# Batch 0's attention by pairs of chunks: other load order, weight-queue gate, and first-GEMM order in a fused attention + MLP kernel

## The chip, the core and the metric

The kernel runs on one core of a Trainium2 chip. The core has five engines, each with its own instruction queue worked strictly in order: TensorE (PE), VectorE (DVE), ScalarE (ACT), GpSimd (POOL) and SyncE (SP). Transfers between HBM and on-chip memory (SBUF) are done by 16 DMA engines; SP, ACT and POOL issue them. Matmul results land in PSUM, from where DVE or ACT copy them to SBUF.

The metric is the device time of one execution in microseconds. Before the change it is 290.98 us, the median of 13 runs (290.07 to 292.09).

## What is computed

```python
# q, k, v: (8 batches, 8 heads, 576 positions, 64), float32
q_s = exp(q - max) / sum over the 64 features
k_s = exp(k - max) / sum over the 576 positions
kv  = einsum('bhsd,bhse->bhde', k_s, v)
att = einsum('bhsd,bhde->bhse', q_s, kv)
x   = att.transpose(0, 2, 1, 3).reshape(4608, 512)
h   = x @ w_in            # 512 x 2048
out = maximum(0.01*h, h) @ w_out   # 2048 x 512
```

A linear attention: the softmax of q runs over features, that of k over positions, so each head needs only a 64 x 64 matrix `kv`. Its output feeds a two-layer MLP with a leaky ReLU.

## The kernel before

**Layout.** The four chunks `g` (0 to 3) of q, k and v hold two heads each: 128 partitions (two heads x 64), and in each partition nine groups `r` of 64 values, which are consecutive rows of the sequence. A pair of chunks, `gp` = 0 or 1, is the unit of most steps. The MLP works on nine token tiles `t` of 512 tokens (`TT`), batches have 576, so a batch always spans two tiles; batch 0's last 64 columns belong to tile 1.

**Attention of one batch**, per pair: `make_exp` (L157) takes the exponential of q or k on ACT; `make_qnorm` (L176) sums, inverts and scales q on DVE; `make_transpose` (L203) turns q with 64 x 64 matmuls on PE into a PSUM tile `pt` and copies it to `qT`; `make_vcast` (L167) casts v to bf16 with a column of ones beside it; `make_kv` (L225) sums k^T v over the nine groups in PSUM and then divides by k's sum (its inner `finish`, L241, two DVE instructions) into `kd`; `make_out` (L271) multiplies `kd` with `qT` and copies the result as columns of `xT`, the transposed input of the MLP.

**The MLP of one tile**, `emit_moe` (L429): first GEMM, 64 matmuls of 128 x 128 by 128 x 512 at L379 (16 blocks `j` of the hidden dimension, four contraction blocks `cb` each), two `j` to a PSUM tile `ph`, which ACT turns into `g_sb` with the leaky ReLU (L434); second GEMM, 64 matmuls at L388, into `pout`; a DVE copy (L405) and stores on SP's queue (L399). For tile 0 the first four `j` are done with `cb` outermost, and the second GEMM with `j` outermost, so that each quarter of `w_out` is only needed when its turn comes.

**Order.** Everything is written out by hand: each engine executes its instructions in the order in which the program emits them. `first_attn` (L329) prepares batch 0; then tiles follow. Pieces of the next batch's attention are put into `slots_of(t)` (L481): key (1, j) stands after block `j` of the first GEMM, key (2, ..) after a block of the second. `dummies` (L149) are matmuls on zeros, into a scratch tile, that keep PE active in the opening.

**Loads.** Batch 0 comes on SP's queue in six half loads (L84): q, k, v, each first chunks 0 and 1, then 2 and 3. All weights come on POOL's queue, which also casts them from float32 to bf16 on the way; the small copy `gate` (L128) holds that queue until the last half of k is there. Behind it stand four quarters of `w_in` (by 512 columns), then batch 1's q, two quarters of `w_out`, batch 1's k, a quarter of `w_out`, batch 1's v, the last quarter of `w_out`, and batch 2. Batches 3 to 7 are loaded on SP's queue, behind the stores of an earlier tile. PSUM is one pool of four double banks (`pair`, L70), used in turn.

Of the kernel before, what the change touches and what calls it, by code (L numbers as in the profile page):

```python
# [18 lines left out]
def kernel(  # L19
# [57 lines left out]
    def new_ld(st):  # L77
        for nm in "qkv":
            st[nm] = ld_pool.tile([P, NG, R * D], FP32, name=f"{nm}_ld", tag="ld")

    def load(eng, st, b, nm, g0=0, g1=NG):
        flat = dram[nm][b].rearrange("h s d -> (h s d)")
        src = flat.rearrange("(g p f) -> p g f", g=NG, p=P)[:, g0:g1, :]
        eng.dma_start(out=st[nm][:, g0:g1, :], in_=src)  # L84

    states = {b: {} for b in range(B)}
    new_ld(states[0])
    for nm in "qkv":
        for g0 in (0, 2):
            load(nc.sync, states[0], 0, nm, g0, g0 + 2)  # L90

    wsrc = const_pool.tile([P, TT], BF16, name="wsrc")
    nc.vector.memset(wsrc, 0.0)  # L93
# [19 lines left out]
    FQ = F // WQ  # L113
    JQ = NF // WQ

    def emit_w_in(i):
        f0, f1 = i * FQ, (i + 1) * FQ
        nc.gpsimd.dma_start(out=w_in_sb[:, :, f0:f1], in_=w_in_r[:, :, f0:f1])  # L118

    def emit_w_out(i):  # L120
        nc.gpsimd.dma_start(
            out=w_out_sb[:, i * JQ : (i + 1) * JQ, :], in_=w_out_r[:, i * JQ : (i + 1) * JQ, :]
        )

    gate = const_pool.tile([P, 1], FP32, name="gate")
    nc.gpsimd.tensor_copy(out=gate, in_=states[0]["k"][:, NG - 1, 0:1])  # L128
    for i in range(WQ):
        emit_w_in(i)  # L130
    new_ld(states[1])
    load(nc.gpsimd, states[1], 1, "q")
    emit_w_out(0)
    emit_w_out(1)
    load(nc.gpsimd, states[1], 1, "k")
    emit_w_out(2)
    load(nc.gpsimd, states[1], 1, "v")
    emit_w_out(3)

    def load_batch(eng, b):  # L140
        new_ld(states[b])
# [58 lines left out]
            for lo in (0, HP):  # L200
                yield par, 2 * gp + par, lo, (HP - lo if par else lo)

    def make_transpose(st, b, gp, r0=0, r1=R, copy=None):  # L203
        def piece():
            if "qT" not in st:
                st["qT"] = qT_pool.tile([P, NG, S], BF16, name="qT")
            pt = pair("pt", BF16)
            for r in range(r0, r1):
                for par, g, lo, to in quads(gp):
                    nc.tensor.matmul(  # L210
                        pt[to : to + HP, par, r * D : (r + 1) * D],
                        lhsT=qe_buf[b % 2][lo : lo + HP, g, r * D : (r + 1) * D],
                        rhs=ident[lo : lo + HP, lo : lo + HP],
                        is_transpose=True,
                        start=(r == r0),
                        stop=(r == r1 - 1),
                    )
            (copy or nc.vector.tensor_copy)(  # L218
                out=st["qT"][:, 2 * gp : 2 * gp + 2, r0 * D : r1 * D],
                in_=pt[:, :, r0 * D : r1 * D],  # L220
            )

        return piece
# [34 lines left out]
    def kv_piece(st, b):  # L258
        return lambda: make_kv(st, b)()()
# [39 lines left out]

        return piece  # L300

    def out_pieces(b, extra=()):
        n1 = TT - (b * S) % TT
        if 2 * n1 <= TT:
            groups = [[(b, gp, 0, n1) for gp in range(NP)]]
            groups += [[(b, gp, n1, S)] for gp in range(NP)]
        else:
            groups = [[(b, gp, 0, n1)] for gp in range(NP)]
            groups += [list(extra) + [(b, gp, n1, S) for gp in range(NP)]]
        return [  # L310
            make_out(parts, (nc.scalar.copy if i == 1 else nc.vector.tensor_copy,))
            for i, parts in enumerate(groups)
        ]
# [12 lines left out]
    def transpose_pieces(b, st):  # L326
        return [make_transpose(st, b, gp) for gp in range(NP)]

    def first_attn(st):  # L329
        b = 0  # L330
        acopy, dcopy = nc.scalar.copy, nc.vector.tensor_copy
        dummies(22)
        make_exp(st, b, "q", 0)()
        make_exp(st, b, "q", 1)()
        make_exp(st, b, "k", 0)()
        make_qnorm(st, b, 0, 0, R - 1)()
        make_qnorm(st, b, 1, 0, R - 1)()
        make_transpose(st, b, 0, 0, R - 1, acopy)()
        dummies(10)
        make_exp(st, b, "k", 1)()  # L340
        make_vcast(st, b, 0, 2, acopy)()
        make_vcast(st, b, 2, 3, acopy)()
        make_transpose(st, b, 1, 0, R - 1)()
        make_vcast(st, b, 3, NG)()
        dummies(3)
        kv0, kv1 = make_kv(st, b, [0]), make_kv(st, b, [1])
        fin0 = kv0()
        dummies(2)
        fin1 = kv1()
        fin0()  # L350
        fin1()
        dummies(2)
        for gp in range(NP):
            make_out([(b, gp, 0, TT)], (acopy, dcopy))()


    def rest_norm(st):
        for gp in range(NP):
            make_qnorm(st, 0, gp, R - 1)()
# [67 lines left out]
                store_rows(eng, t, tsub, lo, out_sb, o0, o1)  # L427

    def emit_moe(t, slots):  # L429
        x = xT.pop(t)  # L430
        g_sb = g_pool.tile([P, NF, TT], BF16, name="g_sb")

        def act(jj, ph):
            nc.scalar.activation(  # L434
                out=g_sb[:, 2 * jj : 2 * jj + 2, :], in_=ph, func=AF.Prelu, alpha=LEAKY_SLOPE
            )

        def run(*key):
            for piece in slots.get(key, ()):
                piece()  # L440

        JJ0 = 2 if t == 0 else 0
        if JJ0:
            phs = [pair("ph") for _ in range(JJ0)]
            for cb in range(NB):
                for j in range(2 * JJ0):
                    gemm1_mm(phs[j // 2], x, j, cb)
            for jj in range(JJ0):
                act(jj, phs[jj])
        for jj in range(JJ0, NF // 2):  # L450
            ph = pair("ph")
            for j in (2 * jj, 2 * jj + 1):
                for cb in range(NB):
                    gemm1_mm(ph, x, j, cb)
                if j % 2:
                    act(jj, ph)
                run(1, j)
        if t == 0:
            pouts = [pair("pout") for _ in range(NTS // 2)]
            for j in range(NF):  # L460
                for tsub in range(NTS):
                    gemm2_mm(pouts[tsub // 2], g_sb, tsub, j)
                run(2, j)
            for i in range(NTS // 2):
                store(pouts[i], t, 2 * i, 2 * i + 2)
        else:
            for tsub in range(NTS):
                if t == NT - 1 and tsub == NTS - 1:
                    last_subtile(g_sb, t, tsub)
                    continue  # L470
                alone = t == NT - 1 and tsub == NTS - 2
                if tsub % 2 == 0:
                    pout = pair("pout")
                for j in range(NF):
                    gemm2_mm(pout, g_sb, tsub, j)
                if tsub % 2 or alone:
                    store(pout, t, tsub if alone else tsub - 1, tsub + 1)
                run(2, tsub)


    def slots_of(t):  # L481
        slots = {}

        def put(key, pieces):
            slots.setdefault(key, []).extend(pieces)

        if t == 0:
            st, st0 = states[1], states[0]
            prep = prep_pieces(1, st)
            tr = transpose_pieces(1, st)  # L490
            outs = out_pieces(1, [(0, gp, TT, S) for gp in range(NP)])
            put((1, 5), [lambda: rest_norm(st0)])
            put((1, 13), prep[0:2])
            put((1, 15), prep[2:4])
            put((2, 4), prep[4:6])
            put((2, 6), [lambda: rest_transpose(st0), tr[0]])
            put((2, 10), prep[6:7])
            put((2, 11), [kv_piece(st, 1), tr[1]])
            put((2, 13), outs[0:2])
            put((2, 14), outs[2:3])  # L500
            return slots
        if t == 1:
            st = states[2]
            prep = prep_pieces(2, st)
            for i in range(7):
                put((1, 2 * i + 1), prep[i : i + 1])
            put((2, 0), transpose_pieces(2, st) + [kv_piece(st, 2)])
            outs = out_pieces(2)
            put((2, 2), outs[0:2])
            put((2, 3), outs[2:3])  # L510
        elif t + 1 < B:
            st = states[t + 1]
            put((1, 2), [kv_piece(st, t + 1)] + transpose_pieces(t + 1, st))
            put((1, 8), out_pieces(t + 1))
        if t + 2 < B:
            prep = prep_pieces(t + 2, states[t + 2])
            put((2, 0), prep[0:4])
            put((2, 1), prep[4:6])
            put((2, 2), prep[6:7])
        return slots  # L520

    first_attn(states[0])
    for t in range(NT):
        if t > 0 and t + 2 < B:
            load_batch(nc.sync, t + 2)
# [31 lines left out]
```

## Time and profile before

| what | value |
|---|---|
| median of 13 runs | 290.98 us (290.07 to 292.09) |
| profiled execution, its own time | 292.09 us |
| its span, first to last instruction | 289.9 us |
| granted TensorE clock, mean | 0.997 of full |
| HBM read, written | 36.70 MB, 9.44 MB |
| first GEMM of tile 0 starts | 16.50 us |
| first GEMM of tile 1 starts | 50.75 us |

Of the profile's words: *busy* is the time in which an engine executes something; *idle before* is its idle time just ahead of an instruction, with the one that ended it named. A "slice" is a fortieth of the span, 7.25 us. The chain of waits follows the work that ended last back to the first instruction, each step to what released it. Matmul ends are modelled: a lone 128 x 512 matmul is shown with 379 ns, though one follows the other every 0.216 us (64 in 13.8). DMA rates count bytes as written, so that weights, cast to half their size, show half the rate at which they are read.

### The profile page before, as it was taken

Reading aid. Unit: us, or ns where it says so; the run is one execution under the profiler, and the core shown is the slowest. Engines: PE = TensorE matmul, PEld = TensorE weight load, DVE = VectorE, ACT = ScalarE, POOL = GpSimd, SP = SyncE. Lnnn points to the kernel's source line nnn. Section 1 sums busy time; section 2 is a strip of 40 time slices with the busy share of each in tenths; the row PEclk is TensorE's granted clock in tenths of the full one; section 3 lists DMA queues with packets and bytes.
Section 4 is the critical chain, followed back from the end, with each engine's and each line's share of the span. In section 5 each row is a group of like instructions: output and inputs, shape, how many; then the busy total and the mean of one; then the engine's idle time right before and its main releaser. Section 6 shows DMA issues by size and latency. Waiting matters only on the chain.

```text
span 289.9 us, 5481 instructions
## 1 busy us (share of the span) xinstructions
PE 277.3 (96%) x2457; PEld 131.1 (45%) x2487; DVE 109.7 (38%) x144; ACT 118.1 (41%) x118; POOL 12.4 (4%) x21
## 2 busy tenths in 40 slices
PE   8879977999999999999999999999999999999994
PEld 3434434445454445444544445444544444444444
DVE  2830744755952283319240933184220200110012
ACT  5645531696126811672157414650461055006400
POOL 0652100000000000000000000000000000000000
PEclk9999999999999999999999999999999999999998
DMA  7899999694169214840494039603300330033014
GB/s 253 275 204 287 276 321 412 150 339 170 29 159 367 87 30 112 300 195 2 116 323 196 2 89 288 262 0 72 75 2 0 72 75 0 0 72 75 0 29 116
DMA packets 21350, 42.29 MB, mean 146 GB/s; under 512 B 1744, under 2 KB 6096, under 8 KB 21328
## 3 DMA queue, kind: packets, MB, share of 16 engines
q1 hardware_dynamic: 15312, 30.55, 34.0%
q0 software_dynamic: 5856, 11.27, 14.9%
q8 instruction: 19, 0.31, 0.4%
q10 hardware_dynamic: 160, 0.13, 0.2%
q14 instruction: 3, 0.02, 0.0%
HBM read 36.70 MB, written 9.44 MB: 159 GB/s over the span
## 4 chain that ended last, share of the span: by engine, by line
PE 83%; DMA 13%; issue 1%; POOL 1%; DVE 1%; SPq 0%
PE ph L379 38%; PE pout L388 38%; DMA v_ld<-in_v_dram 8%; DMA k_ld<-in_k_dram 3%; DMA w_in_sb<-in_moe_w_in_dram 3%; PE pt L210 2%; PE po L279 2%; PE pkv L233 2%; PE pout L417 1%; DVE vb L169 0%; SPq L84 0%; POOL gate L128 0%; POOL w_in_sb L118 0%; DVE out_sb L425 0%
## 5 line engine op out<-in xcount | busy, mean ns | idle before, releaser
L379 PE MATMUL ph<-xT,w_in_sb 128*128 128x512 bf16 x560 | 125.8, 379 | 2.9 <-DMA w_in_sb<-in_moe_w_in_dram 1.5
L434 ACT ACTIVATE g_sb<-ph 128x1024 bf16<-128x1024 f32 x72 | 73.5, 1023 | 128.5 <-PE ph L379 128.5
L388 PE MATMUL pout<-w_out_sb,g_sb 128*128 128x512 bf16 x548 | 122.6, 379 | 2.2 <-DMA w_out_sb<-in_moe_w_out_dram 1.3
L379 PEld LDWEIGHTS <-w_in_sb 128*128 128x128 bf16 x576 | 55.2, 98 | 68.5 <-DMA w_in_sb<-in_moe_w_in_dram 1.9
L388 PEld LDWEIGHTS <-g_sb 128*128 128x128 bf16 x560 | 54.2, 98 | 67.3 <-issue 2.1
L405 DVE COPY out_sb<-pout 128x1024 f32<-128x1024 f32 (+1 forms) x18 | 21.4, 1191 | 78.4 <-PE pout L388 76.2
L184 DVE TENSOR_REDUCE qsum<-qe 128x18 f32<-128x1152 bf16 (+2 forms) x18 | 21.9, 1215 | 46.0 <-ACT qe L159 46.0
L295 DVE CAST xT<-po 128x128 bf16<-128x128 f32 (+7 forms) x23 | 13.6, 637 | 24.3 <-PE po L279 24.3
L186 DVE TENSOR_TENSOR qe<-qe,qrec 128x1152 bf16<-128x1152 bf16 (+2 forms) x18 | 22.0, 1224 | 0.6
L159 ACT ACTIVATE ke<-k_ld 128x1152 bf16<-128x1152 f32 x16 | 17.9, 1154 | 5.2 <-DMA k_ld<-in_k_dram 5.2
L159 ACT ACTIVATE qe<-q_ld 128x1152 bf16<-128x1152 f32 x16 | 18.0, 1156 | 2.5 <-DMA q_ld<-in_q_dram 2.5
L218 DVE COPY qT<-pt 128x1152 bf16<-128x1152 bf16 (+1 forms) x15 | 10.7, 744 | 6.8 <-PE pt L210 6.7
L295 ACT CAST xT<-po 128x896 bf16<-128x896 f32 (+3 forms) x7 | 5.8, 829 | 16.7 <-PE po L279 16.7
L153 PE MATMUL scr<-wsrc 128*128 128x512 bf16 x37 | 10.8, 443 | 1.5 <-DVE wsrc L93 1.2
L169 DVE CAST vb<-v_ld 128x2304 bf16<-128x2304 f32 (+1 forms) x8 | 10.2, 1276 | 4.3 <-DMA v_ld<-in_v_dram 4.3
L210 PE MATMUL pt<-ident,qe 64*64 64x64 bf16 x568 | 7.6, 196 | 0.3 <-DVE qe L186 0.3
L233 PEld LDWEIGHTS <-ke 64*64 64x64 bf16 x576 | 5.6, 106 | 4.3 <-issue 3.8
L210 PEld LDWEIGHTS <-qe 64*64 64x64 bf16 x568 | 6.6, 104 | 1.8 <-issue 1.7
L279 PE MATMUL po<-qT,kd 64*64 64x512 bf16 (+7 forms) x128 | 6.2, 292 | 1.2 <-issue 1.1
L233 PE MATMUL pkv<-vb,ke 64*64 64x65 bf16 x576 | 6.5, 193 | 0.9 <-DVE vb L169 0.7
L153 PEld LDWEIGHTS <-wsrc 128*128 128x128 bf16 x39 | 3.9, 111 | 6.2 <-issue 2.5
L244 DVE RECIPROCAL krec<-pkv 128x4 f32<-128x4 f32 (+1 forms) x9 | 1.6, 177 | 11.8 <-PE pkv L233 11.8
(29 smaller groups left out, 39.5 us busy)
## 6 DMA issues: line engine op xcount, KB each, us to landing
out_dram<-out_sb SPq DMA_DIRECT2D x70, 128.0 KB, 2.4
q_ld<-in_q_dram SPq DMA_DIRECT2D x5, 1152.0 KB, 6.1
k_ld<-in_k_dram SPq DMA_DIRECT2D x5, 1152.0 KB, 8.9
v_ld<-in_v_dram SPq DMA_DIRECT2D x5, 1152.0 KB, 11.3
q_ld<-in_q_dram POOLq DMA_DIRECT2D x2, 1152.0 KB, 18.0
k_ld<-in_k_dram POOLq DMA_DIRECT2D x2, 1152.0 KB, 21.3
v_ld<-in_v_dram POOLq DMA_DIRECT2D x2, 1152.0 KB, 22.4
w_in_sb<-in_moe_w_in_dram POOLq DMA_DIRECT2D x4, 512.0 KB, 8.2
```

Source lines behind the costliest of these rows:

```text
L153: nc.tensor.matmul(scratch["t"][:, 0, :], lhsT=wsrc[:, 0:P], rhs=wsrc, start=True, stop=True)
L159: nc.scalar.activation(out=(qe_buf if nm == "q" else ke_buf)[b % 2][:, 2 * gp : 2 * gp + 2, :], in_=st[nm][:, 2 * gp : 2 * gp + 2, :], fun ...
L184: nc.vector.reduce_sum(out=qsum[:, :, 0:n], in_=x, axis=AX.X)
L186: nc.vector.tensor_tensor(out=x, in0=x, in1=qrec[:, :, 0:n].unsqueeze(3).to_broadcast([P, 2, n, D]), op=ALU.mult,)
L210: nc.tensor.matmul(pt[to : to + HP, par, r * D : (r + 1) * D], lhsT=qe_buf[b % 2][lo : lo + HP, g, r * D : (r + 1) * D], rhs=ident[lo : lo ...
L233: nc.tensor.matmul(pkv[to : to + HP, par, i * VW : i * VW + D + 1], lhsT=ke[lo : lo + HP, g, r * D : (r + 1) * D], rhs=vb[lo : lo + HP, g, ...
L279: nc.tensor.matmul(pos[par % len(pos)][lo : lo + HP, par, at : at + n], lhsT=kd_buf[b % 2][frm : frm + HP, g, :], rhs=states[b]["qT"][frm ...
L295: copies[0](out=dst, in_=pos[0][:, :, at : at + n])
L379: nc.tensor.matmul(ph[:, j % 2, :], lhsT=w_in_sb[:, cb, j * P : (j + 1) * P], rhs=x[:, cb, :], start=(cb == 0), stop=(cb == NB - 1),)
L388: nc.tensor.matmul(pout[:, tsub % 2, :], lhsT=g_sb[:, j, tsub * P : (tsub + 1) * P], rhs=w_out_sb[:, j, :], start=(j == 0), stop=(j == NF ...
L405: nc.vector.tensor_copy(out=out_sb[:, k0:k1, :], in_=pout[:, k0:k1, :])
L434: nc.scalar.activation(out=g_sb[:, 2 * jj : 2 * jj + 2, :], in_=ph, func=AF.Prelu, alpha=LEAKY_SLOPE)
```

## The change

Five things are edited together. (1) Batch 0 is loaded as q, q, k, v, k, v, so that chunks 0 and 1 of k and v come ahead of chunks 2 and 3. (2) `first_attn` takes pair 0 through to its columns of `xT` before pair 1's kv: the casts, copies and dummies are reordered, both qT copies are DVE's, pair 1's transposes are emitted ahead of pair 0's `make_out`, with their copy behind it (`before`), and pair 1's kv and out become slots of tile 0. (3) Tile 0's first four blocks run in halves of the contraction: `cb` 0 and 1 (pair 0) for all four blocks, then `cb` 2 and 3. Pair 1's kv stands before the first of these matmuls, its out after the first four. (4) The gate waits for the first half of k, where it waited for the second; `w_in`'s first quarter becomes two DMAs of 256 columns each, two quarters of `w_out` go ahead of batch 1's q, batch 1's k and v stand next to each other, and the last quarter of `w_out` becomes two DMAs behind them. (5) The slots of tile 0 in which batch 1 is prepared are moved; the remaining columns of batch 0 are a `make_out` of their own, and the last out piece of batch 1 goes to tile 1.

```diff
-    for nm in "qkv":
-        for g0 in (0, 2):
-            load(nc.sync, states[0], 0, nm, g0, g0 + 2)
+    for nm, g0 in (("q", 0), ("q", 2), ("k", 0), ("v", 0), ("k", 2), ("v", 2)):
+        load(nc.sync, states[0], 0, nm, g0, g0 + 2)
...
-    def emit_w_in(i):
-        f0, f1 = i * FQ, (i + 1) * FQ
+    def emit_w_in(f0, f1):
         nc.gpsimd.dma_start(out=w_in_sb[:, :, f0:f1], in_=w_in_r[:, :, f0:f1])
...
+    def emit_w_out(j0, j1):
+        nc.gpsimd.dma_start(out=w_out_sb[:, j0:j1, :], in_=w_out_r[:, j0:j1, :])
...
-    nc.gpsimd.tensor_copy(out=gate, in_=states[0]["k"][:, NG - 1, 0:1])
-    for i in range(WQ):
-        emit_w_in(i)
+    nc.gpsimd.tensor_copy(out=gate, in_=states[0]["k"][:, 1, 0:1])
+    emit_w_in(0, FQ // 2)
+    emit_w_in(FQ // 2, FQ)
+    for i in range(1, WQ):
+        emit_w_in(i * FQ, (i + 1) * FQ)
     new_ld(states[1])
+    emit_w_out(0, JQ)
+    emit_w_out(JQ, 2 * JQ)
     load(nc.gpsimd, states[1], 1, "q")
-    emit_w_out(0)
-    emit_w_out(1)
+    emit_w_out(2 * JQ, 3 * JQ)
     load(nc.gpsimd, states[1], 1, "k")
-    emit_w_out(2)
     load(nc.gpsimd, states[1], 1, "v")
-    emit_w_out(3)
+    emit_w_out(3 * JQ, 3 * JQ + JQ // 2)
+    emit_w_out(3 * JQ + JQ // 2, NF)
...
+            if before:
+                before()
             (copy or nc.vector.tensor_copy)(
                 out=st["qT"][:, 2 * gp : 2 * gp + 2, r0 * D : r1 * D],
...
         dummies(22)
-        make_exp(st, b, "q", 0)()
-        make_exp(st, b, "q", 1)()
-        make_exp(st, b, "k", 0)()
+        for nm, gp in (("q", 0), ("q", 1), ("k", 0)):
+            make_exp(st, b, nm, gp)()
+        make_vcast(st, b, 0, 2, acopy)()
         make_qnorm(st, b, 0, 0, R - 1)()
         make_qnorm(st, b, 1, 0, R - 1)()
-        make_transpose(st, b, 0, 0, R - 1, acopy)()
-        dummies(10)
+        make_transpose(st, b, 0, 0, R - 1, dcopy)()
+        dummies(7)
+        make_kv(st, b, [0])()()
         make_exp(st, b, "k", 1)()
-        make_vcast(st, b, 0, 2, acopy)()
+        out0 = make_out([(b, 0, 0, TT)], (acopy, dcopy))
+        make_transpose(st, b, 1, 0, R - 1, dcopy, before=out0)()
+        dummies(7)
         make_vcast(st, b, 2, 3, acopy)()
-        make_transpose(st, b, 1, 0, R - 1)()
         make_vcast(st, b, 3, NG)()
-        dummies(3)
-        kv0, kv1 = make_kv(st, b, [0]), make_kv(st, b, [1])
-        fin0 = kv0()
-        dummies(2)
-        fin1 = kv1()
-        fin0()
-        fin1()
-        dummies(2)
-        for gp in range(NP):
-            make_out([(b, gp, 0, TT)], (acopy, dcopy))()
+        return [lambda: make_kv(st, b, [1])()(), make_out([(b, 1, 0, TT)], (acopy, dcopy))]
...
-            for cb in range(NB):
-                for j in range(2 * JJ0):
-                    gemm1_mm(phs[j // 2], x, j, cb)
+            order = [(cb, j) for j in range(4) for cb in (0, 1)]
+            order += [(cb, j) for j in range(4) for cb in (2, 3)]
+            for i, (cb, j) in enumerate(order):
+                run(0, i)
+                gemm1_mm(phs[j // 2], x, j, cb)
...
-            outs = out_pieces(1, [(0, gp, TT, S) for gp in range(NP)])
-            put((1, 5), [lambda: rest_norm(st0)])
-            put((1, 13), prep[0:2])
-            put((1, 15), prep[2:4])
-            put((2, 4), prep[4:6])
-            put((2, 6), [lambda: rest_transpose(st0), tr[0]])
-            put((2, 10), prep[6:7])
-            put((2, 11), [kv_piece(st, 1), tr[1]])
-            put((2, 13), outs[0:2])
-            put((2, 14), outs[2:3])
+            put((0, 0), first[0:1])
+            put((0, 4), first[1:2])
+            put((1, 7), [lambda: rest_norm(st0)])
+            put((2, 0), prep[0:6] + [make_vcast(st, 1, 0, 2, nc.scalar.copy)])
+            put((2, 8), [lambda: rest_transpose(st0), tr[0]])
+            put((2, 11), [tr[1], make_vcast(st, 1, 2, NG)])
+            put((2, 12), [make_out([(0, gp, TT, S) for gp in range(NP)]), kv_piece(st, 1)])
+            put((2, 13), out_pieces(1)[0:2])
...
-            put((2, 0), transpose_pieces(2, st) + [kv_piece(st, 2)])
+            put((2, 0), out_pieces(1)[2:3] + transpose_pieces(2, st) + [kv_piece(st, 2)])
...
-    first_attn(states[0])
+    first = first_attn(states[0])
```

More of the change, by code (lines that the diff above doesn't have):

```diff
@@ L114 @@
     JQ = NF // WQ
-    def emit_w_in(i):
-        f0, f1 = i * FQ, (i + 1) * FQ
+    def emit_w_in(f0, f1):
         nc.gpsimd.dma_start(out=w_in_sb[:, :, f0:f1], in_=w_in_r[:, :, f0:f1])
[L120 to L123, printed above, removed]
+    def emit_w_out(j0, j1):
+        nc.gpsimd.dma_start(out=w_out_sb[:, j0:j1, :], in_=w_out_r[:, j0:j1, :])
     gate = const_pool.tile([P, 1], FP32, name="gate")
-    nc.gpsimd.tensor_copy(out=gate, in_=states[0]["k"][:, NG - 1, 0:1])
-    for i in range(WQ):
-        emit_w_in(i)
+    nc.gpsimd.tensor_copy(out=gate, in_=states[0]["k"][:, 1, 0:1])
[3 more added lines that the diff above has]
+        emit_w_in(i * FQ, (i + 1) * FQ)
     new_ld(states[1])
+    emit_w_out(0, JQ)
+    emit_w_out(JQ, 2 * JQ)
     load(nc.gpsimd, states[1], 1, "q")
-    emit_w_out(0)
-    emit_w_out(1)
+    emit_w_out(2 * JQ, 3 * JQ)
     load(nc.gpsimd, states[1], 1, "k")
-    emit_w_out(2)
     load(nc.gpsimd, states[1], 1, "v")
-    emit_w_out(3)
+    emit_w_out(3 * JQ, 3 * JQ + JQ // 2)
+    emit_w_out(3 * JQ + JQ // 2, NF)
     def load_batch(eng, b):
@@ L201, in quads, with make_transpose @@
                 yield par, 2 * gp + par, lo, (HP - lo if par else lo)
-    def make_transpose(st, b, gp, r0=0, r1=R, copy=None):
+    def make_transpose(st, b, gp, r0=0, r1=R, copy=None, before=None):
         def piece():
@@ L300, in make_out, with out_pieces @@
         return piece
-    def out_pieces(b, extra=()):
+    def out_pieces(b):
         n1 = TT - (b * S) % TT
@@ L308, in out_pieces @@
             groups = [[(b, gp, 0, n1)] for gp in range(NP)]
-            groups += [list(extra) + [(b, gp, n1, S) for gp in range(NP)]]
+            groups += [[(b, gp, n1, S) for gp in range(NP)]]
         return [
@@ L429, in emit_moe @@
     def emit_moe(t, slots):
-        x = xT.pop(t)
+        x = xT[t]
         g_sb = g_pool.tile([P, NF, TT], BF16, name="g_sb")
```

## The prediction

> **What bounds the kernel now.** I read the page's first two parts, then PE's timeline, then the chain of waits.
>
> ```profile
> PE 277.3 (96%) x2457; PEld 131.1 (45%) x2487; DVE 109.7 (38%) x144; ACT 118.1 (41%) x118; POOL 12.4 (4%) x21
> PE   8879977999999999999999999999999999999994
> DMA  7899999694169214840494039603300330033014
> ...
> ```
>
> PE is busy 96% of the span; in the 40 slices its only digits below 9 before the last are in the first seven (0 to 51 us), where the 16 DMA engines are nearly full. So there are two regimes: from about 51 us PE never waits and the end is a fixed amount of PE work away; before that, loads decide. What the change is worth is therefore **how much earlier the second token tile's first GEMM starts**, 50.75 us now, less what later stages gain in work. PE's timeline before that point (start, duration, operation, idle before it and its cause):
>
> ```profile
> 16.50 13.99 PE L379 MATMUL ph<-xT,w_in_sb 128*128 128x512 bf16 x62 [1.51 <-DMA w_in_sb<-in_moe_w_in_dram]
> ...
> 39.50 3.61 PE L388 MATMUL pout<-w_out_sb,g_sb 128*128 128x512 bf16 x16 [1.15 <-DMA w_out_sb<-in_moe_w_out_dram]
> 43.77 0.78 PE L233 MATMUL pkv<-vb,ke 64*64 64x65 bf16 x72 [0.66 <-DVE vb L169]
> ...
> 49.64 0.30 PE L279 MATMUL po<-qT,kd 64*64 64x128 bf16 x6 [1.13 <-issue]
> ...
> 50.75 13.98 PE L379 MATMUL ph<-xT,w_in_sb 128*128 128x512 bf16 x62
> ```
>
> Four losses: 1.5 us for the first w_in quarter, 1.15 for the third w_out quarter, 0.66 for batch 1's v, and 1.13 for xT copies and their PSUM buffers. The chain, in time order, gives the loads' side:
>
> ```profile
> 2.25 7.46 DMA k_ld<-in_k_dram
> ...
> 9.77 1.20 POOL gate L128
> 10.97 0.82 POOL w_in_sb L118
> 11.78 7.28 DMA w_in_sb<-in_moe_w_in_dram
> ...
> 19.34 22.89 DMA v_ld<-in_v_dram
> 42.26 1.37 DVE vb L169
> ```
>
> The weights are issued only after all of k has landed (9.71). In quarter-microsecond windows the loads of batch 0 run at 380 to 430 GB/s to 11.25 and fall to 4 GB/s by 12.5; weights begin at 12.5 and average 102 GB/s to 13.75; from 14 they write 205 GB/s of bf16, which is 410 of fp32 read. So from 14 to 51 the DMA stream is full, at about 0.41 MB/us of fp32, and one hole of some 1.5 us lies ahead of it.
>
> **The change, part by part.**
>
> *Gate.* The third load on SP's queue (first half of k) landed at 8.2: its exponential starts at 8.25 after waiting for it. SP's order now is q, q, k, v, k, v, of equal size, so by the slots' present times (8.2, 9.7, at most 11.3, 12.5) v's first half comes at 9.7 and k's second at 11.3. The gate runs 8.25 to 9.45 and everything on POOL behind it, all issues, moves 1.4 to 1.5 us forward. The present delay from issue (10.91) to flow (12.5) is 1.6; now 9.45 gives 11.05, where SP's queue still has 0.22 MB to move. The hole closes: I take **1.4 us** for the stream. Sharing may delay v's second half by up to 0.5 (0.22 MB at half rate against its present tail), hidden, since DVE and ACT reach it only at 13.9 and 13.1 (below).
>
> *w_in in halves.* Same bytes, one more issue (0.77 to 0.88 us, faster than the 1.28 its 0.52 MB take), but 1024 rows of 512 B written in place of 512 of 1 KB. No row shows that size. Below, nothing (rate by bytes: 2,304-byte rows of q, k, v and 2-KB reads of weights both run near 410 GB/s); above, a fixed price per row, doubling w_in's first quarter: +2.56 us. The Trainium skill, "DMA: Bandwidth & Descriptors", Rules for kernel authors, speaks against it: DMAs of at least 1 MiB for rate. By its fit (Anatomy of one DMA: about 2.0 us fixed and 436 GB/s) a further DMA alone would add 2.0 us. But w_in's quarters follow each other at 205 GB/s without a gap: here the fixed part overlaps. Its Specifications put the line rate at 512 B and more; the new rows are just on it. I take 0 and keep 2.56 for the range.
>
> *POOL beside DVE.* The skill's "SBUF — State Buffer" (SBUF: two separate sides) warns that VectorE's two-port copies lock GpSimd out of writing descriptors. Issues beside busy DVE here take 0.77 to 0.88, with idle DVE 0.74 to 0.76; full blocking would add each copy's 0.7. I follow the row: nothing.
>
> *First attention.* The chain now, with present durations: DVE's two q norms end at 10.92; qT copy 0.69 → 11.64; v's first half is cast on ACT 9.75–10.9, so kv of pair 0 (0.48) ends at 11.45 and the pair-1 transposes follow; reciprocal and scaling 0.5 → 12.15; two-by-two out matmuls 0.3 → 12.45; xT copy on DVE 0.65 → 13.25; qT copy of pair 1 0.7 → 13.95; cast of v's last quarter 0.75 → 14.7; kv of pair 1 0.5 → 15.2. Seven dummies (1.5) fit in 12.45 to 13.96. The qT copy taken from ACT (0.99) goes onto DVE, which sets this chain: 0.7 on the path. The first GEMM starts at **15.2**, with pair 1's out (0.3) after four matmuls, against 16.50. The halves of the contraction cost no matmul. w_in lands at about 13.5 and 14.8 (needed 15.2 and 16.4), the others 1.4 earlier than now (19.1, 21.8 and 25.3, where POOL's waits on them end), so 17.7, 20.4 and 23.9, needed at 19.0, 22.4 and 25.9: no stall. 64 matmuls at 0.216 = 13.8: the GEMM ends at 29.33.
>
> *w_out and batch 1.* By position in the stream: third w_out 39.45 − 1.4 − 2.88 (batch 1's k, now behind it) = 35.2, needed at 36.3. q gets two w_out quarters ahead (5.1 us): about 32, so exponentials to 34.3, norms (3.0 each) to 36.2 and 39.2; transposes are reached at 37.1 and 40.4. k: 36.85 + 2.56 − 1.4 = 38.0. v: 42.24 − 1.4 = 40.85, then casts to 42.4 (ACT's 1.14; DVE's half behind a qT copy). The last w_out ends where it did: 42.24 + 2.56 = 44.8, now 43.4, its first half **42.1**.
>
> *Second GEMM.* From 29.33: 36 matmuls 7.78 → 37.11; rest and first transposes 0.73; 12 matmuls 2.59; second transposes 0.55 → 40.98. Then the wait is w_out's half: 42.1, 1.1 us. What follows is 16 matmuls (3.45), rest out 0.3, kv 0.65, outs 0.57: 4.98 → **47.1**. v's cast is 0.6 ahead of its use, outs no longer stand twice in a row before the GEMM, and 8 matmuls cover their copies (1.09), so the 1.13 goes.
>
> *Later.* One out piece moves into the second tile: 0.3. PE's order behind it is the same to the end. Batch 2 lands 1.4 earlier while its use comes 3.7 earlier: q at about 46, ACT reaches it at 49.6; k at 49 against 56: covered.
>
> Sum: 50.75 − 47.1 − 0.3 = **3.35 us**. The profiled execution took 292.09 (span 289.9, 2.2 around it): 288.7. It was the highest of 13, 1.1 above their median; from 290.98 the forecast is **287.6**.
>
> **Rivals.**
> - *The last w_out half isn't late* (0.10). PE goes on at 40.98: 45.96, gain 4.5: 286.5. For: I have its landing only as "before 44.87", where PE took it without a wait. Against: v, measured, precedes it.
> - *Narrow rows cost per row* (0.13). +2.56 on the stream eats the 1.4: w_out's half at 44.7, start 49.65, gain 0.8: 290.2. Against it: rates that follow bytes.
> - *Slower: 512-byte writes run far under line rate* (0.05). Place: w_in's first quarter, everything on POOL behind it. The tile start moves one for one with the stream, since w_out's half already decides; it is slower than before from a loss of 3.4 us. A quarter of the rate would cost 7.7: 290.98 − 3.35 + 7.7 = 295.3. For it only that the size is on the limit.
> - *It doesn't do what it says* (0.04): SP's tail and the early weights only exchange bandwidth, v's second half slips by the gain, and the ACT and DVE queues hold the rest: 291.
>
> **The numbers.** The forecast's own case (0.68) spans 286.6 to 288.6, by ±1 us in the landing lag. The range, 286.2 to 290.2, takes in the first rival and all but the dear end of the second. A difference of 0.2% (0.6 us) is what a measurement tells from none. Faster by more: 0.68 + 0.10 + 0.11 of the second rival, 0.89; same, the rest of it and the last rival, 0.06; slower 0.05.
>
> **What would show it.** Gate ending near 9.5; no hole in the DMA rate at 11.5 to 13.75; first GEMM at 15.2 without a DMA wait; a wait of about 1 us for w_out near 41; second tile at 47.1. A wait for w_in after the fourth or eighth matmul, or under 200 GB/s written near 12 to 14, would say that the rows are dear; a wait for v or q near 37 to 43, that landings lag more than by position.

## The result, and the profile after

The changed kernel takes **287.46 us**, the median of 11 runs (287.24 to 287.86). The kernel before, over 48 runs, has a median of 290.84 (289.94 to 292.09). The ratio is 0.9881, with a 95% interval of 0.9867 to 0.9895: 3.4 us faster, where 287.6 us had been forecast from 290.98. The scatter shrank too, from 2.1 us to 0.6.

Not all of this lies in the span from the first to the last instruction, which is on record beside the time. Outside it stand 2.15 us of each execution of the kernel before and 1.8 us of each of the changed one, steady to within 0.1 us. So 0.4 us of the gain comes from outside the span, where neither the prediction nor any experiment looks; its cause is open.

The profiled execution took 287.27 us with a span of 285.5. The page's first parts and its chain by engine, and the chain's line from the page before:

```profile
span 285.5 us, 5479 instructions
...
PE 276.1 (97%) x2454; PEld 131.0 (46%) x2484; DVE 109.4 (38%) x145; ACT 118.8 (42%) x118; POOL 12.9 (5%) x23
...
PE   8799999999999999999999999999999999999994
...
DMA  7999999980397036903492149404200330032014
...
PE 92%; DVE 4%; DMA 1%; issue 1%; ACT 0%
```

```profile
PE 83%; DMA 13%; issue 1%; POOL 1%; DVE 1%; SPq 0%
```

Below 9, PE now has two digits at the start in place of five among the first seven; the dip in the second DMA digit has gone. DMA, 13% of the chain before, is 1%. PE's timeline (start, duration, operation, idle before it):

```profile
14.40 0.47 PE L234 MATMUL pkv<-vb,ke 64*64 64x65 bf16 x34 [0.31 <-DVE vb L168]
14.81 1.04 PE L376 MATMUL ph<-xT,w_in_sb 128*128 128x512 bf16 x4
15.77 0.41 PE L280 MATMUL po<-qT,kd 64*64 64x512 bf16 x4
16.12 13.12 PE L376 MATMUL ph<-xT,w_in_sb 128*128 128x512 bf16 x58
29.08 7.93 PE L385 MATMUL pout<-w_out_sb,g_sb 128*128 128x512 bf16 x36
...
40.55 1.04 PE L385 MATMUL pout<-w_out_sb,g_sb 128*128 128x512 bf16 x3
...
45.78 13.98 PE L376 MATMUL ph<-xT,w_in_sb 128*128 128x512 bf16 x63
...
64.31 0.78 PE L234 MATMUL pkv<-vb,ke 64*64 64x65 bf16 x72 [0.23 <-DVE xT L296]
```

From 14.81 to tile 1 no row waits for a transfer: the waits for w_in, for w_out's third quarter and for batch 1's v are gone, and so is the 1.13 before the last out piece. Tile 1 starts 4.97 us earlier than in the execution profiled before, the span is 4.4 shorter. Nearly all of the 0.57 between them is the out piece moved into tile 1 (0.31) and a wait new with it, 0.23, ended by a copy of `xT`; that the copy was holding a PSUM buffer is inferred from the code.

### The profile page after: what moved, and what is told of

The parts are those of the page before. It is cut to its first block, busy times and chain, and to the rows that moved or that the text cites. A ratio compares the mean times of both kernels' runs of the same rounds, so it can differ in the third digit from the quotient of the medians.

```text
span 285.5 us, 5479 instructions
## 1 busy us (share of the span) xinstructions
PE 276.1 (97%) x2454; PEld 131.0 (46%) x2484; DVE 109.4 (38%) x145; ACT 118.8 (42%) x118; POOL 12.9 (5%) x23
## 4 chain that ended last, share of the span: by engine, by line
PE 92%; DVE 4%; DMA 1%; issue 1%; ACT 0%
PE ph L376 44%; PE pout L385 42%; PE po L280 2%; PE pkv L234 2%; PE pt L209 2%; PE pout L414 1%; DMA q_ld<-in_q_dram 1%; DVE qe L185 1%; DVE qsum L183 1%; DVE qT L219 1%; DVE vb L168 0%; ACT qe L158 0%; DVE xT L296 0%; DVE xT L299 0%; DVE qrec L184 0%
## 5 line engine op out<-in xcount | busy, mean ns | idle before, releaser
L219 DVE COPY qT<-pt 128x1152 bf16<-128x1152 bf16 (+1 forms) x16 | 11.3, 738 | 1.5 <-PE pt L209 1.5
L152 PE MATMUL scr<-wsrc 128*128 128x512 bf16 x34 | 9.6, 442 | 1.5 <-DVE wsrc L92 1.2
L168 DVE CAST vb<-v_ld 128x2304 bf16<-128x2304 f32 (+2 forms) x8 | 9.6, 1198 | 0.0
```

The costliest lines, as they stand in the source:

```text
L152: nc.tensor.matmul(scratch["t"][:, 0, :], lhsT=wsrc[:, 0:P], rhs=wsrc, start=True, stop=True)
L219: (copy or nc.vector.tensor_copy)(out=st["qT"][:, 2 * gp : 2 * gp + 2, r0 * D : r1 * D], in_=pt[:, :, r0 * D : r1 * D],)
```

## The experiments

Each ratio compares a run with executions of the kernel before that were taken beside it; their median went from 290.7 to 291.45. All versions fall into two groups by the time outside the span: 2.15 us in the kernel before, the gate alone, the middle without the opening and the two runs with DVE's chain shortened, 1.8 in all others. Why is not known. So differences of half a microsecond are read from the median spans, which for the changed kernel is 285.75 us.

**The kernel before, profiled again.** No edit.

> The kernel before, unchanged, profiled a second time. Theory A (its profiled execution, 292.09 us, was 1.1 above its median because loads landed late in that one): this span is shorter than 289.9, about 288.8, and the first GEMM of tile 1 starts about 1 us before 50.75, with batch 1's v landing before 42.2. Theory B (the execution shown was typical up to 50.75 us, and the spread arises elsewhere): tile 1 again starts within 0.3 us of 50.75.

292.01 us, span 289.8, tile 1 at 50.58, v's cast at 42.2 again. Theory A fell: a second execution shows the same waits. But the two profiled executions both lie at the top of a range of 290 to 292; what the quick ones look like, they do not show.

**The gate alone**, in the kernel before:

```diff
-    nc.gpsimd.tensor_copy(out=gate, in_=states[0]["k"][:, NG - 1, 0:1])
+    nc.gpsimd.tensor_copy(out=gate, in_=states[0]["k"][:, 1, 0:1])
```

> The kernel before with one edit: the gate waits for the first half of k. Theory A (the stream of weights moves forward by the hole that it closes, about 1.4 us, and everything up to tile 1 is bound by it): first GEMM about 0.35 us earlier, held by xT at 16.1; waits for w_out and v shrink; tile 1 starts 1.4 earlier; 289.4 us. Rival (the first GEMM and the two out pieces bind, loads hardly): 290.5 or more.

289.59 us, ratio 0.9945 (0.9923 to 0.9967); median span 287.4, where the executions of before beside it have 289.3; tile 1 at 48.26. About half of the gain or more comes from this one index, and more than expected. Two views say why. First the timeline around the gate, before and in this run (start, duration, operation):

```profile
9.70 1.22 DVE L186 TENSOR_TENSOR qe<-qe,qrec 128x1024 bf16<-128x1024 bf16 x1
9.77 1.20 POOL L128 COPY gate<-k_ld 128x1 f32<-128x1 f32 x1 [8.46 <-DMA k_ld<-in_k_dram]
```

```profile
8.09 1.21 DVE L184 TENSOR_REDUCE qsum<-qe 128x16 f32<-128x1024 bf16 x1
...
8.15 0.18 POOL L128 COPY gate<-k_ld 128x1 f32<-128x1 f32 x1 [6.85 <-DMA k_ld<-in_k_dram]
```

The same copy of one column takes 1.20 us beside a DVE multiplication with two SBUF inputs, and 0.18 beside a reduction with one. In the first case it ends 0.05 after the multiplication does (10.92, 10.97). In the changed kernel it takes 0.26, from 7.96 to 8.22, where the multiplication ends at 8.18; in the next run, the opening without the middle, 0.54, to 8.28 where that ends at 8.23; in the repeat of before 1.11, ending at 11.07 where that ends at 11.03. Four lengths, each ending 0.04 to 0.05 after DVE does: in the profiled executions of before, the gate was mostly a wait for DVE. This is what the Trainium skill, "SBUF — State Buffer" (SBUF: two separate sides), says: a DVE operation with two SBUF inputs and a GpSimd operation that reads SBUF exclude each other for a whole instruction.

Second, one-microsecond windows (the last two columns are the DMA engines' busy share and GB/s), before and then in this run:

```profile
11.00:12.00 1.00, 1.00 (x36) 0.58 (x35) 0.42 (x1) 1.00 (x2) 1.00 (x2) 1.00 0.52 203
12.00:13.00 1.00, 0.75 (x38) 0.58 (x38) 0.71 (x2) 0.87 (x2) 1.00 (x2) 1.00 0.38 67
13.00:14.00 1.00, 0.89 (x38) 0.48 (x38) 0.71 (x4) 0.23 (x1) 1.00 (x3) 1.00 0.89 128
...
23.00:24.00 1.00, 1.00 (x6) 0.48 (x5) 0.00 (x0) 0.38 (x1) 0.00 (x0) 1.00 1.17 355
```

```profile
11.00:12.00 1.00, 1.00 (x36) 0.54 (x35) 0.50 (x1) 1.00 (x2) 1.00 (x2) 1.00 1.19 271
12.00:13.00 1.00, 0.70 (x38) 0.58 (x38) 0.74 (x2) 0.84 (x2) 1.00 (x3) 1.00 1.21 192
13.00:14.00 1.00, 1.00 (x39) 0.48 (x38) 0.74 (x4) 0.12 (x1) 1.00 (x2) 1.00 1.24 205
...
21.00:22.00 1.00, 1.00 (x7) 0.47 (x5) 0.00 (x0) 0.78 (x2) 0.74 (x1) 1.00 1.19 314
```

The hole is closed: from 11 us on, until w_in has passed, no window of one microsecond is under 192 GB/s. Batch 1's q, uncast and so counted at twice the rate, follows w_in in both; its rise marks the place in the stream: within 23 to 24 before, within 21 to 22 now. From the mix of 205 and 410 GB/s in these windows, the step is estimated at 23.3 and 21.5. At this place the stream moved by about 1.8 us, where 1.4 had been taken.

**The opening without the middle.** The changed kernel with POOL's queue behind w_in and tile 0's slots of before:

```diff
+    load(nc.gpsimd, states[1], 1, "q")
     emit_w_out(0, JQ)
     emit_w_out(JQ, 2 * JQ)
-    load(nc.gpsimd, states[1], 1, "q")
-    emit_w_out(2 * JQ, 3 * JQ)
     load(nc.gpsimd, states[1], 1, "k")
+    emit_w_out(2 * JQ, 3 * JQ)
     load(nc.gpsimd, states[1], 1, "v")
-    emit_w_out(3 * JQ, 3 * JQ + JQ // 2)
-    emit_w_out(3 * JQ + JQ // 2, NF)
+    emit_w_out(3 * JQ, NF)
...
-            put((1, 7), [lambda: rest_norm(st0)])
+            put((1, 5), [lambda: rest_norm(st0)])
...
```

> The change's opening (load order, gate on the first half of k, w_in's first quarter in two, pair 0 first, first GEMM in halves of the contraction) with the queue behind w_in and tile 0's slots as before. Theory A (opening 1.3 us, the middle the rest): first GEMM at 14.8, waits for w_out's third quarter and v remain at about 1 us together, the 1.1 us before the last out piece too; 289.3 us. Rival (all of the gain is in the earlier opening): 287.5.

289.13 us, ratio 0.9927 (0.9906 to 0.9949). The first GEMM starts at 14.98; the waits for v (0.64) and ahead of the last out piece (1.12) are back, that for w_out is not; tile 1 at 48.27. The waits are as theory A had them. But nothing is gained over the gate alone: the median spans are 287.35 and 287.4, tile 1 starts at 48.27 and 48.26, and the 0.5 us between the times is within the intervals and lies outside the span. The first GEMM's earlier start (15.87 with the gate alone) is lost again by the time batch 1's v is there: its kv starts at 41.31 in both.

**The middle without the opening.** The changed kernel with load order, first attention and first-GEMM order of before, but the early gate:

```diff
-    for nm, g0 in (("q", 0), ("q", 2), ("k", 0), ("v", 0), ("k", 2), ("v", 2)):
+    for nm, g0 in (("q", 0), ("q", 2), ("k", 0), ("k", 2), ("v", 0), ("v", 2)):
...
-            order = [(cb, j) for j in range(4) for cb in (0, 1)]
-            order += [(cb, j) for j in range(4) for cb in (2, 3)]
+            order = [(cb, j) for cb in range(NB) for j in range(4)]
...
-            put((0, 0), first[0:1])
-            put((0, 4), first[1:2])
```

> The change with its opening undone: load order, first attention and first-GEMM order as before; gate on the first half of k, w_in's first quarter in two, queue and slots as changed. Theory A: first GEMM at about 16.1, no wait behind it, so about 1.0 us slower than the changed kernel: 288.5 us. Rival (the opening gives nothing, since loads decide anyway): 287.5.

288.02 us, ratio 0.9891 (0.9867 to 0.9916): within the interval of the whole change. The median span is 285.85, 0.1 us above the changed kernel's; the rest of the difference in time lies outside the span. The old order of the first attention starts its GEMM like this, and meets one wait for a transfer behind it:

```profile
15.47 13.97 PE L383 MATMUL ph<-xT,w_in_sb 128*128 128x512 bf16 x62 [0.46 <-ACT xT L299]
...
41.12 1.02 PE L392 MATMUL pout<-w_out_sb,g_sb 128*128 128x512 bf16 x3 [0.30 <-DMA w_out_sb<-in_moe_w_out_dram]
```

15.47, not the 16.1 expected: the first matmuls need only the first quarter of xT, not the last copy. The new order starts at 14.81, but an out piece still interrupts its GEMM; the second GEMM starts at 29.28 here and at 29.08 in the changed kernel. So doing pair 0 first and the GEMM in halves of the contraction gives 0.2 us there, 0.3 at tile 1 (46.08 and 45.78), 0.1 in the median span. The rival, that loads decide anyway, was nearer than theory A. The early gate, w_in's halves and the middle make up nearly all of the gain in the span.

**The gate on the last half of k**, in the changed kernel:

```diff
-    nc.gpsimd.tensor_copy(out=gate, in_=states[0]["k"][:, 1, 0:1])
+    nc.gpsimd.tensor_copy(out=gate, in_=states[0]["k"][:, NG - 1, 0:1])
```

> The changed kernel with the gate back on the last half of k, which now lands as the fifth load, at 10.8. Theory A (the gate closes the hole between batch 0's loads and the weights; the stream moves by the hole and the first GEMM is within 0.2 us of it): a hole of 1.5 to 2 us returns at 11.5, w_in's second quarter comes about 1.7 later, PE waits for it about 1.5; 289.0 us. Rival (batch 0's last loads and the early weights only exchange bandwidth): 287.5, v's second half lands earlier and kv of pair 1 starts earlier.

290.73 us, ratio 1.0008 (0.9985 to 1.0031): the whole gain is gone, more than both theories had. PE's timeline and windows of the profiled execution, which took 291.97 us (the third column from the end is the granted clock):

```profile
16.47 1.04 PE L376 MATMUL ph<-xT,w_in_sb 128*128 128x512 bf16 x4 [1.48 <-DMA w_in_sb<-in_moe_w_in_dram]
...
19.17 0.61 PE L376 MATMUL ph<-xT,w_in_sb 128*128 128x512 bf16 x1 [1.32 <-DMA w_in_sb<-in_moe_w_in_dram]
```

```profile
15.00:16.00 1.00, 0.00 (x0) 0.00 (x0) 0.46 (x2) 0.00 (x0) 1.00 (x2) 1.00 0.92 103
...
18.00:19.00 1.00, 0.00 (x0) 0.00 (x0) 0.96 (x3) 0.46 (x1) 0.00 (x0) 1.00 1.24 194
19.00:20.00 1.00, 0.61 (x2) 0.29 (x4) 0.90 (x5) 0.00 (x0) 0.60 (x1) 0.59 1.24 205
20.00:21.00 1.00, 1.00 (x3) 0.45 (x3) 0.06 (x1) 0.00 (x0) 0.16 (x1) 0.50 1.24 208
```

Two waits for w_in, 2.8 us together, stand 1.4 us apart, and then TensorE's granted clock falls to half from about 19.2 until about 22.5. That is a price on top of the waits: of its 12 runs the five with a mean clock of 0.998 or more have a median of 290.26, the seven at 0.991 to 0.994 one of 291.29. From 14 to 17 us the weights also flowed at about half their rate (103 GB/s in the first of the windows); why, no run here tells.

**w_in's first quarter in one DMA**, in the changed kernel:

```diff
-    emit_w_in(0, FQ // 2)
-    emit_w_in(FQ // 2, FQ)
+    emit_w_in(0, FQ)
```

> The changed kernel with w_in's first quarter as one DMA. Theory A (halving lets the first matmuls start before the second half is there, and its narrow rows cost next to nothing): the first GEMM waits for w_in until about 15.7 where it started at 14.8; 288.3 us. Rival (the narrow rows cost more than the early half saves): 287.4 or less.

287.95 us, ratio 0.9912 (0.9889 to 0.9935). The median span is 286.2, 0.45 us above the changed kernel's, and tile 1 starts 0.5 later (46.29). But PE waits for w_in only 0.16 us, until 15.32. The rest of the later start stands ahead of it: pair 1's kv starts at 14.68, not at 14.40, behind a later cast of pair 0's v. So of the 0.8 us expected of halving, the trace shows 0.2 as a wait for w_in; whether the later cast comes from the undivided DMA, it doesn't show.

**All of w_in in halves**, in the changed kernel:

```diff
-    for i in range(1, WQ):
-        emit_w_in(i * FQ, (i + 1) * FQ)
+    for i in range(2, 2 * WQ):
+        emit_w_in(i * FQ // 2, (i + 1) * FQ // 2)
```

> The changed kernel with all four quarters of w_in in halves of 256 columns: four times the narrow rows. Theory A (a quarter in narrow rows costs at most 0.25 us of stream): q of batch 1 begins to flow at most 0.8 later, time 287.5 to 287.9 us. Rival (a fixed price per row, 2.56 us for each quarter): 7.7 us more of stream, PE waits for every later quarter; over 292 us.

287.86 us, ratio 0.9905 (0.9882 to 0.9928). Windows of this run, and then of the changed kernel:

```profile
14.00:16.00 2.00, 1.69 (x44) 0.78 (x41) 0.82 (x3) 0.00 (x0) 1.07 (x2) 1.00 1.33 179
16.00:18.00 2.00, 1.46 (x10) 0.61 (x8) 1.62 (x6) 0.58 (x1) 0.98 (x2) 1.00 1.39 182
18.00:20.00 2.00, 2.00 (x11) 0.93 (x10) 0.38 (x2) 1.38 (x2) 1.26 (x2) 1.00 1.44 194
20.00:22.00 2.00, 2.00 (x11) 0.90 (x10) 0.00 (x0) 1.35 (x2) 0.94 (x2) 1.00 1.45 196
```

```profile
14.00:16.00 2.00, 1.69 (x44) 0.78 (x41) 0.81 (x3) 0.00 (x0) 1.69 (x3) 1.00 1.26 203
16.00:18.00 2.00, 1.95 (x12) 0.90 (x10) 1.63 (x6) 0.58 (x1) 0.06 (x1) 1.00 1.24 205
18.00:20.00 2.00, 2.00 (x11) 0.88 (x9) 0.37 (x2) 1.94 (x2) 0.75 (x1) 1.00 1.24 205
20.00:22.00 2.00, 2.00 (x11) 0.93 (x10) 0.00 (x0) 1.02 (x1) 0.70 (x1) 1.00 1.24 204
```

Where the changed kernel writes rows of 1 KB at 203 to 205 GB/s, this run writes rows of 512 B at 179 to 196, 188 on the mean: 8% less, an estimated 0.2 us on a quarter. In the trace batch 1's q lands 1.0 us later (ACT's exponential of it, after a wait, at 32.10 and not at 31.12), and PE waits 0.49 us for w_in at 16.68 and 0.31 for w_out at 41.49. A fixed price per row, and with it two rivals, are ruled out: 7.7 us of stream had been due.

**POOL's queue in the old order**, in the changed kernel, slots kept (the lines of the queue in the diff under "The opening without the middle", with the last quarter of w_out still in two):

> The changed kernel with POOL's queue behind w_in in the order of before: batch 1's q ahead of w_out, k ahead of w_out's third quarter, v ahead of the last. Theory A (by position in the stream, w_out's first quarter comes 2.9 later, at about 29.3, its third about as PE reaches it): waits of 0.3 and up to 0.8 us for w_out, 288.2 us. Rival (the order hides anyway): 287.5.

288.42 us, ratio 0.9924 (0.9904 to 0.9945), median span 286.6, 0.85 above the changed kernel's, and the expected row:

```profile
37.06 1.02 PE L385 MATMUL pout<-w_out_sb,g_sb 128*128 128x512 bf16 x4 [0.83 <-DMA w_out_sb<-in_moe_w_out_dram]
```

Counting transfers' places in the stream held here, for w_out's third quarter; its first did not come late.

**The multiplication beside the gate in four**, in the kernel before:

```diff
-            nc.vector.tensor_tensor(
-                out=x,
+            for g0, g1 in ([(0, 2)] if split == 1 else [(0, 1), (1, 2)]):
+                for a, z in cuts:
+                    nc.vector.tensor_tensor(
+                        out=x[:, g0:g1, a:z, :],
...
-        make_qnorm(st, b, 1, 0, R - 1)()
+        make_qnorm(st, b, 1, 0, R - 1, split=4)()
```

> The kernel before with one edit: the multiplication of pair 1's q norm is four DVE instructions of 256 columns in place of one of 1024 (1.22 us). Theory A (the gate's copy on POOL takes 0.18 us by itself and its 1.20 us were a wait for that multiplication to end, which begins at 9.70, just as k lands at 9.71): the gate now takes at most 0.6 us, the weights are issued 0.6 us or more earlier, about 290.2 us, although DVE has three instructions more. Rival (the copy takes 1.2 us when it waits for the last half of k, whatever DVE does): gate 1.2 us, time 290.8.

290.41 us, ratio 0.9986 (0.9970 to 1.0002): not to be told from no change; the median spans are 288.65 here and 288.6 before. The trace doesn't test the lock as meant, but shows its other side:

```profile
9.38 0.18 POOL L128 COPY gate<-k_ld 128x1 f32<-128x1 f32 x1 [8.07 <-DMA k_ld<-in_k_dram]
```

In this execution k had landed by 9.38 while the multiplications began only at 9.90; the gate slipped in ahead, ended at 9.56 where it ended at 10.97 before, and tile 1 started at 49.45, not at 50.75. So in the kernel before, whether the gate costs 0.2 or 1.2 us depends on which of two events, a few tenths of a microsecond apart, comes first. That could account for much of its 2 us of scatter, and for two profiled executions at the upper end: this one, with the gate free, has a span of 288.7, about the median of the executions of before beside it (288.6). It isn't shown, as only profiled executions show the gate.

**DVE's chain shortened**, in the changed kernel:

```diff
-        out0 = make_out([(b, 0, 0, TT)], (acopy, dcopy))
+        out0 = make_out([(b, 0, 0, TT)], (acopy, acopy))
...
-        make_vcast(st, b, 2, 3, acopy)()
-        make_vcast(st, b, 3, NG)()
+        make_vcast(st, b, 2, NG)()
```

> The changed kernel with work moved off the chain of DVE that sets its first GEMM's start: both halves of pair 0's xT copy on ACT, v's chunks 2 and 3 cast by DVE in one instruction. Theory A (DVE's chain sets the start at 14.8, and behind it w_in's second quarter, landing at 18.4, is only 0.2 us from being late): kv of pair 1 starts up to 0.9 us earlier, the GEMM then waits for w_in's second quarter, 287.2 us. Rival (loads are not next in line): 286.6. Against both: the cast of 1152 columns takes 1.2 us instead of 0.75 while POOL issues DMAs, and nothing is gained.

287.68 us, ratio 0.9891 (0.9868 to 0.9914): nothing gained in time; the median span, 285.5, is 0.25 us shorter, within the scatter of either. The cast of 1152 columns took 1.02 us, between the two figures, and the seven dummies, which PE executes in order, ended at 14.2, after the cast (13.81). So they held kv. With four in place of seven:

> As the run before it (both halves of pair 0's xT copy on ACT, v's chunks 2 and 3 cast by DVE in one instruction), with four dummies in place of seven ahead of pair 1's kv, which in that run stood behind the seventh. Theory A (loads are next in line): kv of pair 1 starts 0.4 us earlier and the GEMM then waits for w_in's second quarter, landing 18.4 to 18.9, by about as much; 287.4 us, no different from the changed kernel. Rival (the dummies alone held it): 287.0 or less.

287.90 us, ratio 0.9888 (0.9865 to 0.9911), median span 285.7. The first GEMM starts at 14.40 and does not wait for w_in; the wait comes later:

```profile
40.62 1.02 PE L384 MATMUL pout<-w_out_sb,g_sb 128*128 128x512 bf16 x4 [0.41 <-DMA w_out_sb<-in_moe_w_out_dram]
```

Theory A was right that loads are next in line and wrong about which: it is w_out's last quarter. The 0.4 us gained at 14.4 are lost there; tile 1 starts at 45.59, 0.2 earlier than in the changed kernel, because batch 1's kv takes 0.78 us and not 1.04. No version here has a lower time than the changed kernel.

## Why the prediction was right, and where not

**The gate and the stream** were the right mechanism, mis-sized. The gate was priced at 1.2 us, its own duration in the trace; it takes 0.18 where DVE leaves it free and had waited for DVE, whose multiplication of 9.70 to 10.92 is in the same trace. Of the lock, which the prediction did weigh, it took only the case of DMA issues, where it indeed costs little, and not the gate itself. The first half of k also landed 0.3 earlier than was taken, the gate ended at 8.22 and not at 9.45, and the stream moved by 1.8 us (w_in's end, with the gate alone) and not by 1.4.

**Narrow rows** at no cost: by the rate in the run with all of w_in in halves, 0.2 us on a quarter, near enough.

**The first GEMM** was to start at 15.2 and started at 14.81. But this was put down to DVE's chain. The gate alone brings 16.50 down to 15.87, still behind a wait for w_in; with w_in's first quarter in halves the old order starts at 15.47; and the new order's 14.81, less what its interrupted GEMM gives back, is worth 0.2 more. So most of the term came from loads. The 0.1 to 0.3 us that the new order is worth in the end is less than the 1.0 that was taken for it (16.50 to 15.2, less an out piece of 0.3).

**w_in's later quarters** were to have 1.3 us to spare. POOL's wait, which ends at 18.39, shows the second there by then, not at 17.7, for a use at about 18.7 (16.12 and twelve matmuls of 0.216): 0.3 us to spare.

**A wait of 1.1 us for w_out's last quarter near 41** is the step that failed. There is none, which was the first rival, with tile 1 at 45.96; 45.78 is measured. The landing of its first half was taken as 42.1, from v's present one less 1.4. It was there by 40.55, when PE used it without a wait, and k and v, which ACT takes up after a wait, landed earlier too:

```profile
36.48 2.22 ACT L158 ACTIVATE ke<-k_ld 128x1152 bf16<-128x1152 f32 x2 [3.14 <-DMA k_ld<-in_k_dram]
39.27 1.15 ACT L168 CAST vb<-v_ld 128x1152 bf16<-128x1152 f32 x1 [0.58 <-DMA v_ld<-in_v_dram]
```

For k 38.0 had been due, for v 40.85; v landed 3.0 earlier than before. Quarter-microsecond windows put the end of v's flow at an estimated 40.0 before and 38.0 now: 0.6 of the missing 1.6 us is the stream. The other 1.0 is the landing's lag behind the end of the flow, 2.3 us before and 1.3 now. It varies between versions with the same bytes ahead (v lands at 39.85 in the middle without the opening), and why, the runs do not show. The place itself was right: where w_out's half landed a little later, PE waited for it, 0.30 us in that run, 0.31 with all of w_in in halves, 0.45 and 0.41 with DVE's chain shortened. What failed is the size, 1.1.

**Later stages:** 0.3 had been taken, 0.57 measured, for the wait that came with the out piece.

**The sum** in the profiled execution was to be 3.35 and was 4.4 in the span: 1.1 more for the wait that isn't there and 0.4 for reaching its place earlier, less 0.25 between that place and tile 1 and 0.3 later. In time it was 4.8, with the 0.4 outside the span, which had been taken as unchanged. That 287.6 met 287.46 all the same is luck: the execution profiled before stood 1.25 us above its median (292.09 against 290.84), and the one after 0.2 below its own. The gain was taken from such an execution and subtracted from the median, and the two errors, each a little over 1.4 us, cancelled. The direction, the place of the gain and its order of size were right by their reasons; the last microsecond and a half was not.

**The rivals.** Slower by narrow rows is excluded. That early weights only exchange bandwidth is too: the gate alone gives 1.6 us. A slower end was nearer than was thought, by another way: with the gate late, waits of 2.8 us and half a clock give back everything.

## What to carry to other kernels

A row's duration on GpSimd may be a wait: before it is moved at its price, look at what DVE executes in the same span, and whether the row ends with it. One index in the gate of a full queue was worth as much as the whole reordering of loads and slots behind it, because the hole ahead of the stream delayed every later load; reordering the engines' work ahead of the first GEMM, while loads decided, was worth 0.1 to 0.3 us. And a gain worked out in one execution belongs to that execution: where runs scatter by 2 us, find out first where in the scatter the profiled one stands, and how much of a time lies outside its span.

## What the runs showed of the hardware that was not expected

- A one-column copy on GpSimd: 0.18 us when free; 0.26, 0.54, 1.11 and 1.20 when it met a DVE multiplication with two SBUF inputs, ending 0.04 to 0.05 after it each time.
- The granted TensorE clock fell to 0.50 for about 3.4 us after two idle stretches of 1.5 and 1.3 us, with 1.4 us of work between them (the late gate in the changed kernel). Single ones of 1.5 and 1.7 us, in the two profiled executions of the kernel before, left it at 1.00.
- A DVE cast of 1152 columns from fp32 took 0.75 us with POOL idle (changed kernel, at 41.35) and 1.02 and 1.09 while POOL issued DMAs (the two runs with DVE's chain shortened); one of 576 columns took 0.74 in the second case.
- DMA writes of weights, cast to bf16: 203 to 205 GB/s in rows of 1 KB, 179 to 196 in rows of 512 B.
